# Packing the 257-column spectral units of a fused FFT-filter and GEGLU kernel into 256 columns, with bursts of four and new hooks

## The chip, the cores and the metric

One NeuronCore of one Trainium2 chip. The metric is device microseconds of one execution, median of several. All comparisons are of runs in the fast state, except where said (granted clock 0.997 to 1.0 in the runs recorded as fast, 0.756 to 0.991 in those recorded as slow). In the profiles PE is TensorE (PEld its weight loads), DVE is VectorE, ACT ScalarE, POOL GpSimd and SP SyncE; L612 is line 612 of the kernel.

## The reference

```python
x  = A_x                                   # (1, 2048, 512) bf16
xn = layernorm(x)                          # over the last axis
X  = rfft2(xn, axes=(-2, -1))              # 2048 x 257 complex
y  = irfft2(X * (w_r + 1j * w_i), s=(2048, 512))
g, u = xn @ w_gate, xn @ w_up              # 512 -> 1792
return x + y + (gelu(g) * u) @ w_down      # 1792 -> 512
```

## The kernel before

It is written engine by engine. A helper `op` appends an instruction to an engine's queue and works out the semaphore waits from named reads and writes. TensorE's program is the GEGLU (gate, up and down projections, in four blocks of 512 tokens). At fixed places between its matmul groups stand *hooks*, numbered 0 to 159, and a plan says which other work is issued at which hook. A hook is half a gate/up pair (0.86 us of PE) or a third of a down projection (1.0 us).

The filter is done by matmuls against DFT matrices, in 16 units at each of six stages. D transforms the feature axis. A does 64 points of the token axis, on two halves of 64 rows. A goes to a scratch array in DRAM and comes back as `tv`, transposed. B does 32 points, with two halves of 64 columns. VectorE multiplies by the filter. C transforms back, on 64-row halves, and goes through DRAM again to `vv`. E and F finish. A unit of A, B or C has 257 complex columns, so it takes two PSUM banks (the program's banks are 512 fp32 columns wide) and the units go in bursts of two.

```python
def load_tv(j):                                    # scratch -> tv, waits for scr1[j] to land
    dma("sp", tv[j::16], scr1[8*j:8*j+8, :].rearrange("p (x c) -> p x c", c=KD), r=[("scr1", j)], w=[("tv", j)])

def unit_C(h):                                     # unit_A and unit_B are alike
    bk = take(2, 0.3)                              # two neighbouring PSUM banks
    y = yy[h % 4]
    def fn(e):
        for ri in range(2):
            for hh in range(2):                    # two 64-row halves of the array, side by side
                ins = e.matmul(bank(bk + hh)[:, 0:257], cm[64*hh:64*hh+64, h, ri, :], y[64*hh:64*hh+64, ri, 0:KD],
                               start=(ri == 0), stop=(ri == 1), skip_group_check=True)
        return ins
    op("pe", fn, r=[("cm", h), ("yy", h % 4, 0), ("yy", h % 4, 1)], w=[("ps", bk), ("ps", bk + 1)])
    op("act", lambda e: e.activation(v4[:], pair(bk), ACT.Copy), r=[("ps", bk), ("ps", bk + 1)], w=[("vp", h % 4)])
    dma("sp", scr2...[h], v4[:], ...)              # and load_vv(h - 2) right behind it
    ...                                            # cut
# ... cut: column 256 of vv by a matmul of its own (unit_row), 32 x 64, a small DMA and 16 POOL copies

for m in range(1, 4):                              # layernorm, transposes, folds of block m
    a = (2, 14, 23)[m - 1]
    t = (13, 23, 33)[m - 1]
    for i in range(4):
        at(a + i, (ln_stat, 4*m + i))              # VectorE, needs x of the block
    at(a + 3, (ln_aggr, 4*m, 4))
    for i in range(4):
        at(a + 5 + i // 2, (ln_norm, 4*m + i))     # VectorE -> xn
    at(t, (trans, m, (0, 1), ...)); at(t + 1, (trans, m, (2, 3), ...))   # PE, needs xn
    at(t + 2, (butter, m, 0)); at(t + 3, (butter, m, 1))                 # the folds, VectorE, for D
for j in range(NJ):
    h = (9, 11, 13, 15, 19, 21, 23, 25, 28, 30, 31, 33, 38, 39, 40, 41)[j]
    at(h, (unit_D, j))
    if j % 2:
        at(h + 2, (unit_A, j - 1), (unit_A, j))
for i in range(0, 16, 2):
    at(57.5 + 2.6*i, (unit_B, i), (unit_B, i + 1))
    at(65.3 + 2.6*i, (unit_C, i), (unit_C, i + 1))
at(117, (unit_row,))
for j in range(NJ):
    at(117 + 2.25*j, (unit_E, j)); at(121 + 2.25*j, (unit_F, j))
```

## Time and profile before

| | before |
|---|---|
| time, median (lowest to highest) of three runs | 192.27 us (191.92 to 192.29) |
| span of the profile | 190.6 us |
| PE busy / DVE / ACT | 96% / 63% / 47% |

The page of the kernel before: the busy time of each engine with its share of the span and its instructions, and the shares of the chain of work that ended last.

```profile
PE 182.7 (96%) x1170; PEld 93.0 (49%) x1184; DVE 120.3 (63%) x316; ACT 88.6 (47%) x162; POOL 27.2 (14%) x54
...
PE 87%; DVE 5%; DMA 3%; issue 1%; SPq 1%; POOL 1%; ACT 0%; DVEq 0%
```

TensorE bounds the kernel (busy 96% of the span, 87% of the chain that ended last): only what takes a slot on PE or makes PE wait counts. The list of PE's waits (microseconds in total, times, longest):

```profile
PE ps L347 <- DVE gl L316: 1.2, 1, 1.2
PE ps L375 <- DVE xn L365: 1.1, 2, 0.6
PE ps L612 <- DMA wu<-in_B_w_up_dram: 0.9, 1, 0.9
PE ps L415 <- DVE arena L401: 0.6, 1, 0.6
PE ps L654 <- DVE m_1 L476: 0.2, 1, 0.2
PE ps L654 <- DVE hT L618: 0.2, 1, 0.2
```

The first and third lines, and half of the second, are the start. Waits come later: a D unit (L415) at 30.95 us for the fold, and the transposes of the third block (L375) at 35.83 us for `xn`. In the timeline of PE (columns are explained below; in brackets the idle time before, and what ended it):

```profile
30.95 0.23 PE L415 MATMUL ps<-fd,arena 128*128 128x128 f16 x1 [0.63 <-DVE arena L401]
35.83 0.56 PE L375 MATMUL ps<-ident,xn 128*128 128x128 f16 x7 [0.59 <-DVE xn L365]
```

The timeline of PE around a C burst. Columns: start in us, length in us, line, operation, result and inputs, stationary tile, shape, count.

```profile
119.52 1.03 PE L612 MATMUL ps<-xnT,wu 128*128 128x512 f16 x4
120.48 0.62 PE L490 MATMUL ps<-yy,cm 64*128 64x257 bf16 x8
121.03 1.04 PE L597 MATMUL ps<-xnT,wg 128*128 128x512 f16 x4
```

Read the starts here, not the lengths. A 512-column matmul follows another after 216 ns, so four take 0.86 us; from the first to the second line are 0.96 us. The eight matmuls of the burst are four side-by-side pairs of 257 columns, about 0.44 us at the 110 ns from one pair to the next; they take 0.55 us. Entering and leaving the 64-row mode costs about 0.1 us each time. In the trace's own nanoseconds it is 93 to 100 in all 24 bursts: an entry makes the slot of a 512-column matmul 309 to 312 instead of 216, an exit that of a burst's last matmul 201 to 206 instead of 106 (two exits read longer). The list of waits shows none of it.

### The profile page before, as it was taken

The numbers are of one execution on the slowest core, as the hardware profiler recorded it, in microseconds if no ns is written. First come the engines' busy times: TensorE is split into PE (matmuls) and PEld (weight loads), VectorE is DVE, ScalarE is ACT, GpSimd is POOL, SyncE is SP. The second block draws the span as 40 slices with busy tenths as digits, with TensorE's granted clock in tenths as the row PEclk, the third lists the DMA queues.
The fourth block names the chain that finished last, engine by engine and source line by source line (L and its number), as shares of the span: only waits on it lengthen the run. The fifth ranks groups of instructions, "written<-read, shape, count | busy, mean of one in ns | idle before, by whom it ended". The sixth has DMA issues, their size and how long they took to land.

```text
span 190.6 us, 3253 instructions
## 1 busy us (share of the span) xinstructions
PE 182.7 (96%) x1170; PEld 93.0 (49%) x1184; DVE 120.3 (63%) x316; ACT 88.6 (47%) x162; POOL 27.2 (14%) x54
## 2 busy tenths in 40 slices
PE   7699998899999999999999999999999999999993
PEld 2376554455555444444444444444445555555562
DVE  3679849888562142777557646723424969697781
ACT  1344555556447322355636364433225665646410
POOL 2300210417331000222230000000001110111100
PEclk9999999999999999999999999999999999999999
DMA  4999998366998850126765242235000222212112
GB/s 124 280 270 378 214 239 226 128 162 159 232 173 179 186 153 7 39 65 114 161 151 141 79 113 79 73 99 138 3 1 0 57 59 53 59 41 63 37 28 55
DMA packets 20239, 22.96 MB, mean 120 GB/s; under 512 B 2176, under 2 KB 18048, under 8 KB 19840
## 3 DMA queue, kind: packets, MB, share of 16 engines
q1 hardware_dynamic: 17056, 16.69, 33.2%
q0 software_dynamic: 1712, 5.22, 12.8%
q10 hardware_dynamic: 1456, 0.85, 1.6%
q8 instruction: 9, 0.15, 0.3%
q14 instruction: 6, 0.05, 0.1%
HBM read 16.44 MB, written 6.31 MB: 119 GB/s over the span
## 4 chain that ended last, share of the span: by engine, by line
PE 87%; DVE 5%; DMA 3%; issue 1%; SPq 1%; POOL 1%; ACT 0%; DVEq 0%
PE ps L597 24%; PE ps L654 24%; PE ps L612 24%; DMA wu<-in_B_w_up_dram 3%; PE ps L464 2%; PE ps L490 2%; PE ps L524 2%; PE ps L553 2%; PE ps L375 2%; PE ps L634 2%; PE ps L439 1%; SPq L304 1%; DVE hT L618 1%; DVE st L353 1%; PE ps L443 1%
## 5 line engine op out<-in xcount | busy, mean ns | idle before, releaser
L618 DVE TENSOR_TENSOR hT<-ps,gl 128x512 bf16<-128x512 f32 (+1 forms) x60 | 38.8, 651 | 34.1 <-PE ps L612 32.9
L612 PE MATMUL ps<-xnT,wu 128*128 128x512 f16 (+1 forms) x240 | 58.2, 365 | 0.9 <-DMA wu<-in_B_w_up_dram 0.9
L597 PE MATMUL ps<-xnT,wg 128*128 128x512 f16 (+1 forms) x240 | 58.4, 365 | 0.1
L600 ACT ACTIVATE gl<-ps 128x512 bf16<-128x512 f32 (+1 forms) x60 | 34.1, 569 | 47.1 <-PE ps L597 46.2
L654 PE MATMUL ps<-wd,hT 128*128 128x512 bf16 x196 | 47.4, 379 | 1.0 <-DVE m_1 L476 0.2
L612 PEld LDWEIGHTS ps<-xnT,wu 128*128 128x128 bf16 x240 | 22.3, 98 | 22.1 <-DMA wu<-in_B_w_up_dram 1.2
L597 PEld LDWEIGHTS ps<-xnT,wg 128*128 128x128 bf16 x240 | 22.4, 98 | 21.5 <-issue 1.9
L654 PEld LDWEIGHTS ps<-wd,hT 128*128 128x128 bf16 x210 | 19.5, 98 | 22.4 <-issue 1.7
L669 DVE TENSOR_TENSOR x_sb<-ps,x_sb 128x512 bf16<-128x512 f32 x12 | 8.2, 687 | 12.1 <-PE ps L654 12.1
L559 ACT ACTIVATE eo<-ps 128x512 bf16<-128x512 f32 x16 | 9.5, 596 | 13.4 <-PE ps L553 13.4
L532 POOL COPY zt<-xn 1x128 bf16<-1x128 bf16 x16 | 4.8, 298 | 75.9 <-DMA xn<-row 44.8
L353 DVE BATCH_NORM_STATS2 st<-x_sb 128x6 f32<-128x512 bf16 x16 | 10.8, 685 | 3.6 <-DMA x_sb<-in_A_x_dram 3.6
L422 ACT ACTIVATE xs<-ps 128x512 f16<-128x512 f32 x16 | 9.6, 598 | 7.5 <-PE ps L418 7.5
L470 ACT ACTIVATE xc<-ps 128x514 f16<-128x514 f32 x16 | 8.7, 600 | 8.0 <-PE ps L464 8.0
L449 ACT ACTIVATE tt<-ps 128x514 f16<-128x514 f32 x16 | 8.7, 598 | 7.6 <-PE ps L443 7.6
L496 ACT ACTIVATE vp<-ps 128x514 bf16<-128x514 f32 x16 | 8.7, 598 | 5.8 <-PE ps L490 5.8
L531 ACT ACTIVATE zt<-ps 128x512 bf16<-128x512 f32 x16 | 9.5, 592 | 0.0
L361 POOL TENSOR_TENSOR rstd<-vpe,mhalf 128x4 f32<-128x4 f32 (+2 forms) x6 | 5.0, 835 | 25.2 <-DVE vpe L360 25.2
L308 POOL DMA_DIRECT2D Wr<-in_A_w_r_dram x8 | 5.0, 629 | 21.7 <-PE ps L612 16.5
L365 DVE TENSOR_SCALAR xn<-x_sb,ag,rstd 128x512 f16<-128x512 bf16 x16 | 6.0, 420 | 2.3 <-POOL rstd L361 2.3
L385 DVE COPY xnT<-ps 128x1024 f16<-128x1024 f16 (+2 forms) x8 | 4.8, 604 | 3.4 <-PE ps L375 3.4
L553 PEld LDWEIGHTS ps<-gm,zt 128*128 128x128 bf16 x64 | 4.9, 98 | 3.8
(65 smaller groups left out, 168.4 us busy)
## 6 DMA issues: line engine op xcount, KB each, us to landing
scr<-tt SPq DMA_DIRECT2D x16, 128.5 KB
tv<-scr SPq DMA_DIRECT2D x16, 128.5 KB
scr<-vp SPq DMA_DIRECT2D x16, 128.5 KB
arena<-scr SPq DMA_DIRECT2D x16, 128.5 KB
out_dram<-osb SPq DMA_DIRECT2D x30, 64.0 KB
x_sb<-in_A_x_dram SPq DMA_DIRECT2D x6, 256.0 KB, 12.6
Wr<-in_A_w_r_dram POOLq DMA_DIRECT2D x8, 128.5 KB, 3.9
Wi<-in_A_w_i_dram POOLq DMA_DIRECT2D x8, 128.5 KB, 4.6
```

Of the source, the lines that this page charges most:

```text
L353: op("dve", lambda e: e.bn_stats(st[:, j, :], x_sb[:, j, :]), r=[("x", j, 0), ("x", j, 1)], w=[("st", j)])
L422: op("act", lambda e: e.activation(x4[:].rearrange("p (a c r) -> p a c r", a=2, r=4), bank(bk).rearrange("p (a r c) -> p a c r", a=2, r=4) ...
L449: op("act", lambda e: e.activation(t4[:], pair(bk), ACT.Copy, scale=SC_A), r=[("ps", bk), ("ps", bk + 1)], w=[("tt", j % 4)])
L470: op("act", lambda e: e.activation(xc[s2][:, :, 0:KD], pair(bk), ACT.Copy, scale=SC_B), r=[("ps", bk), ("ps", bk + 1)], w=[("xc", s2)])
L531: op("act", lambda e: e.activation(z[:], bank(bk).rearrange("p (a c) -> p a c", a=4), ACT.Copy, scale=SC_E), r=[("ps", bk)], w=[zk])
L553: ins = e.matmul(o[:, i // 2, i % 2, :], z[:, i, :], gm[:, i, :], start=(i == 0), stop=(i == 3), skip_group_check=True)
L559: op("act", lambda e: e.activation(o2[:], bank(bk), ACT.Copy), r=[("ps", bk)], w=[ok])
L597: ins = e.matmul(bank(bg)[:, 0:n], wg_sb[:, dc, fc * P:(fc + 1) * P], xnT[:, dc, c0:c0 + n], start=(dc == 0), stop=(dc == 3))
L600: op("act", lambda e: e.activation(gl[k % 3][:, 0:n], bank(bg)[:, 0:n], ACT.Gelu_apprx_tanh), r=[("ps", bg)], w=[("gl", k % 3)])
L612: ins = e.matmul(bank(bu)[:, 0:n], wu_sb[:, dc, fc * P:(fc + 1) * P], xnT[:, dc, c0:c0 + n], start=(dc == 0), stop=(dc == 3))
L618: op("dve", lambda e: e.tensor_tensor(hT[b % 2][:, fc, h0:h0 + n], bank(bu)[:, 0:n], gl[k % 3][:, 0:n], ALU.mult), r=[("ps", bu), ("gl", k ...
L654: ins = e.matmul(bank(bk), hT[b % 2][:, fc, jj * P:(jj + 1) * P], wd_sb[:, fc, :], start=(fc == 0), stop=(fc == NFC - 1))
```

## The change

After the transform of the feature axis, columns 0 and 256 are purely real, so one complex column can carry both, one as its real and one as its imaginary part. The change packs them into one ("kd 0 and 256 as one"): a unit then has 256 columns and fits one PSUM bank, so that A, B and C can go in bursts of four. To multiply the packed column by two different filter values it needs the column at negated frequency: tiny matmuls with a permutation matrix (15 of 2 to 8 columns) and 44 tiny VectorE operations. The row unit goes. Scratch reads get hooks of their own, and the hooks of layernorm, transposes and D move. The change also regroups the loads of the filter and of C's matrices into fewer ones and moves E and F to other hooks. The core of the diff, with cuts:

```diff
-        vp = [sb("vp%d" % i, [P, 2, KD], BF16) for i in range(4)]
+        tp = [sb("tp%d" % i, [P, 2, 2, KW], F16) for i in range(NTP)]      # KW = 256, NTP = 3
...
+        def quad_C(q):
+            bks = [take(1, 0.22) for _ in range(4)]
+            for i in range(0, 4, 2):
+                def fn(e, i=i):
+                    for u in range(2):
+                        for ri in range(2):
+                            for hh in range(2):
+                                ins = e.matmul(bank2(bks[i + hh])[:, u, :], cm[64 * hh:64 * hh + 64, hs[i + u], ri, :],
+                                               y[64 * hh:64 * hh + 64, i + u, ri, :], start=(ri == 0 and u == 0), ...)
+                    return ins
+                op("pe", fn, ..., w=[("ps", bks[i]), ("ps", bks[i + 1])])    # ScalarE is released pair by pair
...
-            a = (2, 14, 23)[m - 1]
-            t = (13, 23, 33)[m - 1]
+            a = (2, 15, 26)[m - 1]
+            t = (13, 25, 34)[m - 1]
...
-            h = (9, 11, 13, 15, 19, 21, 23, 25, 28, 30, 31, 33, 38, 39, 40, 41)[j]
+            h = (9, 11, 13, 15, 20, 22, 24, 26, 30, 32, 33, 34, 40, 41, 42, 43)[j]
             at(h, (unit_D, j))
-            if j % 2:
-                at(h + 2, (unit_A, j - 1), (unit_A, j))
+            if j % 4 == 3:
+                at(h + 2, (units_A, j - 3, 4) if j < 12 else (units_A, 14, 2))
+                for i in range(j - 3, j + 1):
+                    at(h + (7 if j < 12 else 2), (load_tv, i))
+            elif j == 13:
+                at(h + 2, (units_A, 12, 2))
+        for q in range(4):
+            b = CB + BS * q                                  # 59 + 9 q
+            at(b, (quad_B, q))
+            for s in range(4):
+                at(b + 1 + 2 * s, (quad_mul, q, s))
+            at(b + 2, (filter_cols, q))
+            at(b + 6, (quad_neg, q))
+            at(b + 8, (quad_col, q))
+            at(b + CD, (quad_C, q))                          # CD = 12
+            for h in QUADS[q]:
+                at(b + CD + (5 if q < 3 else 0), (load_vv, h))
-        at(117, (unit_row,))
+            at(CE + EF * j, (unit_E, j))                     # 112 + 2.45 j, F four hooks later
```

## The prediction

> **What bounds it now.** TensorE. The first part of the page gives PE 182.7 us busy of a 190.6 us span (96%), DVE 63%, ACT 47%, and the chain that ended last is 87% PE. The clock is full. From the starts in the timeline, back-to-back matmuls follow each other in columns/2.4 GHz plus about 3 ns (216 ns for 512 columns, 56 ns for 128). The view of waits has only 4.2 us for PE in all: 2.9 us in the warm-up and first loads, 0.6 us for the folds (a D unit, 30.95 us), 0.6 us of 1.1 for the layernorm of the third block (transposes at 35.83 us), 0.2 us twice for DVE.
>
> **The hidden cost.** The 64-row (A, C) and 64-column (B) units run as 24 bursts of two units. Each entry (512-column matmul to the next start: 309-312 ns instead of 216) and each exit (203-206 ns instead of about 110) loses 96-99 ns, so about 0.193 us a burst, 4.6 us in all. No wait shows it. [...]
>
> **The change, costed.**
> - 24 bursts become 13 (A: three of four units, two of two; B and C: four each): 11 x 0.193 = -2.1 us on PE.
> - The row unit for column 256 goes: 0.18 us slot plus 0.10 us entry, -0.27 us. Its 16 POOL copies were off the path.
> - 257 -> 256 columns: about -0.03 us.
> - Added: 15 matmuls of 2 to 8 columns, full-array mode. An estimate from the 56 ns slot of a 128-column matmul with its own weights: +0.9 us.
> - Added: 44 tiny DVE ops. At the 150-170 ns of tiny ones here, +7 us of DVE in the B/C stretch, where 9 hooks replace 10.4 per four units: about 9.3 us of DVE work in a 10.4 us period. Off the path, barely.
> - D of the second block one hook later (20 for 19), the third block's transposes two later with its statistics one later: a hook is 0.86 us of PE, so both 0.6 us waits should go: -1.2 us.
> - A 4-unit burst puts 2.2 us of evictions before the next gelu; PE should not notice. A(14,15) sits about one ACT eviction behind D(15): +0.1-0.3 us. Other new bank or DVE waits: allow +0.4 us.
> - tv: last A and first B both move two hooks, keeping the present slack (landed 73.1, used 75.8 us). vv: 14 hooks (about 12.5 us) between last C and first E instead of 16; landing took 8.7 us and I expect about 10. No wait.
>
> Sum: -2.1 -0.3 -1.2 -0.2 (the two DVE waits, partly) +0.9 +0.6 = about -2.3 to -2.5 us.
>
> **Prediction: 189.8 us (range 188.7 to 191.3).** Faster by over 2%: 0.07; within 2%: 0.90; slower: 0.03.
>
> **What would show it.** 13 entries and exits at about 97 ns each and no row unit; PE busy about 180-181 us; the waits on L401's fold and the third block's xn gone from PE's view; tiny matmuls with slots near 56 ns; DVE near 67% with 85-95% in the B/C windows; no DMA among PE's releasers after the start-up; the tail after the last matmul still about 3 us.
>
> **What would make it wrong.** DVE falling behind in B/C so that up-projection banks come late (several PE waits on hT multiplies); bursts of four holding PSUM so that gates wait for ACT; B or E waiting for scratch reads now issued in fours; [...] the layernorm waits merely moving to the fourth block.

Two passages that no trace of this case shows are cut, where marked. "The clock is full" is a granted clock of 1.000 in the profile of before, and the 2.4 GHz is the slope between the two slots named there (160 ns more for 384 more columns). The two allowances for new waits (+0.1-0.3 and +0.4 us) were estimates of mine that no trace or run had shown.

## More of the kernel before

The timeline of VectorE before the first late wait:

```profile
25.06 0.69 DVE L385 COPY xnT<-ps 128x1024 f16<-128x1024 f16 x1 [1.20 <-PE ps L375]
27.15 0.69 DVE L353 BATCH_NORM_STATS2 st<-x_sb 128x6 f32<-128x512 bf16 x1 [1.40 <-DMA x_sb<-in_A_x_dram]
27.76 0.67 DVE L618 TENSOR_TENSOR hT<-ps,gl 128x512 bf16<-128x512 f32 x1
28.35 0.68 DVE L397 TENSOR_TENSOR arena<-xnT 128x1024 f16<-128x1024 f16 x1
28.95 0.68 DVE L398 TENSOR_TENSOR arena<-xnT 128x1024 f16<-128x1024 f16 x1
...
30.48 0.42 DVE L401 TENSOR_TENSOR arena<-arena 128x512 f16<-128x512 f16 x1
```

The first statistic of the third block (L353) stands at hook 14 and waits 1.40 us for its x to land. The fold of the second block (L397 to L401, hooks 15 and 16) stands behind it in the queue though its own data is there.

## The result, and the profile after

| | before | after |
|---|---|---|
| time, median (lowest to highest) of four runs | 192.09 us (191.91 to 192.29) | 187.74 us (187.51 to 188.17) |
| ratio, 95% interval | | 0.9776 (0.9751 to 0.9800) |
| span of the profile | 190.6 us | 185.7 us |

A ratio is the mean time of one kernel's fast runs over that of the other's of the same rounds, so it is not quite the ratio of the medians. The change won 4.35 us; 2.4 us were predicted, and 187.74 lies below the range. It is faster by over 2%, to which the prediction gave 0.07.

The page of the kernel after, the same lines:

```profile
PE 181.3 (98%) x1198; PEld 95.4 (51%) x1198; DVE 124.5 (67%) x360; ACT 87.7 (47%) x161; POOL 16.4 (9%) x29
...
PE 93%; DMA 3%; SPq 1%; DVE 0%; issue 0%
```

The list of PE's waits is down to one line, the wait for the first memset (a write of zeros by VectorE):

```profile
PE ps L364 <- DVE gl L331: 1.2, 1, 1.2
```

The timeline of PE around a C burst, as above. L527 are two of the tiny matmuls.

```profile
107.50 0.18 PE L527 MATMUL ps<-Wr,be 128*128 128x8 bf16 x1
107.53 0.17 PE L527 MATMUL ps<-Wi,be 128*128 128x8 bf16 x1
107.55 1.02 PE L694 MATMUL ps<-xnT,wu 128*128 128x512 f16 x4
108.51 1.05 PE L583 MATMUL ps<-yq,cm 64*128 64x256 bf16 x16
109.49 1.04 PE L679 MATMUL ps<-xnT,wg 128*128 128x512 f16 x4
```

Four units take 0.98 us from entry to exit, plus 0.1 us of the entry: 1.08 us. Twice the burst of two above is 2 x (0.55 + 0.10) = 1.30 us. And a tiny matmul, though recorded with 0.17 us, holds PE for 0.03 us.

The timeline of VectorE in the early stretch:

```profile
25.15 0.68 DVE L414 TENSOR_TENSOR arena<-xnT 128x1024 f16<-128x1024 f16 x1
25.75 0.69 DVE L415 TENSOR_TENSOR arena<-xnT 128x1024 f16<-128x1024 f16 x1
26.99 0.69 DVE L370 BATCH_NORM_STATS2 st<-x_sb 128x6 f32<-128x512 bf16 x1 [0.55 <-DMA x_sb<-in_A_x_dram]
27.60 0.41 DVE L417 TENSOR_TENSOR arena<-arena 128x512 f16<-128x512 f16 x1
27.92 0.42 DVE L418 TENSOR_TENSOR arena<-arena 128x512 f16<-128x512 f16 x1
```

The x of the third block lands as late as before (27 us), but the first half of the fold now stands ahead of the statistic that waits for it, and D and the transposes come later in PE's program.

The load of VectorE in a whole period of B and C, by the view of windows (microseconds, then busy time and instructions of each engine, the granted clock, DMA share and GB/s):

```profile
94.00:105.00 11.00, 11.00 (x79) 5.36 (x79) 8.92 (x33) 5.83 (x12) 0.00 (x0) 1.00 0.39 110
```

VectorE is busy 81% (8.92 of 11.00 us; 85 to 95% were predicted), and PE 100%.

**A ledger of PE.** PE is full, so the time from its first to its last start can be split without a rest, start to start: what a matmul needs when nothing holds it up (0.4167 ns a column + 2.7 ns, the line through the 216 ns of 512 columns and the 56 ns of 128 in these traces, where 256 columns take 109; the tiny matmuls are not on it and are counted by their slots) and what is lost beyond. From the two traces:

| PE, us | before | after | difference |
|---|---|---|---|
| A, B, C units with all entries and exits | 15.60 | 13.17 | -2.43 |
| row unit with its entry | 0.27 | 0 | -0.27 |
| tiny matmuls (15 slots of 26 to 29 ns) | 0 | 0.41 | +0.41 |
| losses of the start, to 13.5 us | 3.64 | 2.96 | -0.68 |
| late waits (795 + 751 + 168 ns) | 1.71 | 0 | -1.71 |
| from the last matmul's start to the end | 3.27 | 3.29 | +0.02 |

The third late wait, 168 ns, stands before a D unit at 43.2 us; the list of waits doesn't show it. The sum is -4.66 us of the 4.88 between the spans. About 0.1 us of the rest is the first matmul after each exit: of 512 columns it holds PE for 225 to 227 ns instead of 216 (19 times before, 12 after), of 128 columns for 66 or 67 instead of 56 (4 and 1); what is left is scattered in small excesses. The medians are only 4.35 us apart: the profiled run of before took 192.7 us, more than any of the four timed ones, and single profiles contain a start that differs by run, which the experiments take up.

### The profile page after: what moved, and what is told of

Read it like the earlier page. It is cut to its first block, busy times and chain, and to the rows that moved or that the text cites. A ratio compares the mean times of both kernels' runs of the same rounds, so it can differ in the third digit from the quotient of the medians.

```text
span 185.7 us, 3290 instructions
## 1 busy us (share of the span) xinstructions
PE 181.3 (98%) x1198; PEld 95.4 (51%) x1198; DVE 124.5 (67%) x360; ACT 87.7 (47%) x161; POOL 16.4 (9%) x29
## 4 chain that ended last, share of the span: by engine, by line
PE 93%; DMA 3%; SPq 1%; DVE 0%; issue 0%
PE ps L694 26%; PE ps L679 26%; PE ps L736 24%; DMA wu<-in_B_w_up_dram 3%; PE ps L461 2%; PE ps L495 2%; PE ps L583 2%; PE ps L608 2%; PE ps L635 2%; PE ps L392 2%; PE ps L716 2%; SPq L319 1%; PE ps L435 1%; PE ps L434 1%; PE ps L432 1%; PE ps L433 0%
## 5 line engine op out<-in xcount | busy, mean ns | idle before, releaser
L736 PE MATMUL ps<-wd,hT 128*128 128x512 bf16 x210 | 49.6, 379 | 0.0
L751 DVE TENSOR_TENSOR x_sb<-ps,x_sb 128x512 bf16<-128x512 f32 x11 | 7.6, 688 | 10.6 <-PE ps L736 10.6
L439 ACT ACTIVATE ring<-ps 128x512 f16<-128x512 f32 x16 | 9.5, 596 | 6.2 <-PE ps L435 6.2
L470 ACT ACTIVATE tp<-ps 128x512 f16<-128x512 f32 x16 | 8.4, 600 | 5.5 <-PE ps L461 5.5
L591 ACT ACTIVATE tp<-ps 128x512 bf16<-128x512 f32 x16 | 8.3, 602 | 3.4 <-PE ps L583 3.4
L501 ACT ACTIVATE ring<-ps 128x512 f16<-128x512 f32 x16 | 8.2, 610 | 0.0
L649 DVE TENSOR_TENSOR eh<-eo 128x256 bf16<-128x256 bf16 x16 | 4.6, 290 | 4.6 <-ACT eo L641 4.4
L364 PE MATMUL ps<-gl 128*128 128x512 bf16 (+1 forms) x17 | 6.1, 516 | 1.2 <-DVE gl L331 1.2
```

The lines of the kernel that those rows point to most:

```text
L439: op("act", lambda e: e.activation(x4.rearrange("p (a c r) -> p a c r", a=2, r=4), bank(bk).rearrange("p (a r c) -> p a c r", a=2, r=4), A ...
L470: op("act", lambda e, i=i, b=b, k=k: e.activation(tp[k][:, b], bank2(bks[i + b]), ACT.Copy, scale=SC_A), r=[("ps", bks[i + b])], w=[("tp", ...
L591: op("act", lambda e, i=i, hh=hh, k=k: e.activation(vp[k][:, hh], bank2(bks[i + hh]), ACT.Copy), r=[("ps", bks[i + hh])], w=[("tp", k, hh)])
L736: ins = e.matmul(bank(bk), hT[b % 2][:, fc, jj * P:(jj + 1) * P], wd_sb[:, fc, :], start=(fc == 0), stop=(fc == NFC - 1))
```

## The experiments

The theory after the result: the gain is on PE alone, namely fewer changes of tiling mode (2.3 us), the hooks (1.7 us or more), and nothing is given back, because tiny matmuls are cheap and nobody waits. The main rival: bursts of four and fewer operations shorten waits of the other engines, and the modes are a side show. Fourteen runs were made (two of them of the unedited kernels), all with the right result.

### The new hooks alone, on the kernel before

```diff
-            a = (2, 14, 23)[m - 1]
-            t = (13, 23, 33)[m - 1]
+            a = (2, 15, 26)[m - 1]
+            t = (13, 25, 34)[m - 1]
-            h = (9, 11, 13, 15, 19, ...)[j]
+            h = (9, 11, 13, 15, 20, ...)[j]          # the list of after
-            at(57.5 + 2.6 * i, ...B...); at(65.3 + 2.6 * i, ...C...)
+            at(59 + 2.6 * i, ...B...);   at(66.8 + 2.6 * i, ...C...)
```

> The kernel before, with only the new hooks for layernorm, transposes and D units (A follows D; B and C one and a half hooks later so that tv keeps its slack). Ledger theory: the three late waits (795, 751 and 168 ns, counted start to start) go, so -1.7 us, about 190.4 us, and no late PE wait is left. The prediction's sizing from the idle column: -1.2 us, about 190.9 us. Rival, that the bursts of four are what removed those waits: no gain, about 192.

Measured: 190.75 us, ratio 0.9914 (0.9843 to 0.9985), so -1.65 us by the ratio and -1.3 us by the medians, on a chip whose runs scattered more. The interval (-3.0 to -0.3 us) holds both sizings, -1.7 and -1.2, so the times don't tell them apart; that there is no gain, as the rival had it, lies outside. In the trace the late losses fall by 1.40 us: 0.31 us are left (169 ns at a D, 143 ns at the fourth block's transposes). The expectation that no late wait is left was a little too good.

This trace also settles the two "waits on DVE" of 0.2 us. In the kernel before, the down projection after a B burst shows nine matmuls where the program has ten there:

```profile
93.34 0.64 PE L464 MATMUL ps<-tv,be 128*64 128x257 f16 x8
94.14 2.11 PE L654 MATMUL ps<-wd,hT 128*128 128x512 bf16 x9 [0.16 <-DVE hT L618]
96.18 0.62 PE L490 MATMUL ps<-yy,cm 64*128 64x257 bf16 x8
96.73 1.04 PE L654 MATMUL ps<-wd,hT 128*128 128x512 bf16 x4
```

9 + 4 = 13 of the 14 matmuls of a down projection. In the trace of this experiment all 14 are recorded (5 + 9), and the burst is left at the usual cost, with no wait:

```profile
91.08 1.24 PE L654 MATMUL ps<-wd,hT 128*128 128x512 bf16 x5
92.25 0.63 PE L464 MATMUL ps<-tv,be 128*64 128x257 f16 x8
92.82 2.12 PE L654 MATMUL ps<-wd,hT 128*128 128x512 bf16 x9
```

The "wait" was one lost record: its excess over the usual exit, 223 ns (220 ns at the other "wait"), is about a 512-column slot (216 ns). In all, the first trace of before shows 196 of the 210 512-column down-projection matmuls.

### The old hooks on the kernel after

The same edit the other way round (B and C keep their hooks).

> The kernel after, with the old hooks for layernorm, transposes and D units. Ledger theory: the late waits return, +1.5 to +1.7 us, about 189.3 us. Rival, that bursts of four removed them: about 187.8 us and no late wait.

Measured: 189.66 us, ratio 0.9860 (0.9786 to 0.9934), near the +1.5 to +1.7 expected (0.9860 against 0.9776 for after, which ran on another chip, is 1.6 us). But only one late loss is back, 757 ns at the third block's transposes; the D unit did not wait, and the start lost 4.08 us where the trace of after had 2.96. That did not fit the picture of fixed losses and led to the pin tested below.

### Tiny matmuls after the bursts, and inside them

```diff
+        def tiny():                                  # four full-array matmuls of 8 columns, result unused
+            bt = take(1, 0.12, 0.1)
+            ... e.matmul(bank(bt)[:, 0:8], ident[:], fd[:, 0:8], start=True, stop=True, ...) x 4
 # first kernel: tiny() right after each of the 11 bursts of four; second: after the burst's first two units
```

> The kernel after, with four full-array matmuls of 8 columns put right after each of the 11 bursts of four: 44 more tiny matmuls, no more mode changes. At the 26-29 ns slots that the trace of after shows: +1.2 us, about 188.9 us. At the 56 ns that the prediction used: +2.5 us, about 190.2 us. Rival, that such work hides off the path: under +0.3 us.

> The same 44 tiny matmuls, but in the middle of each of the 11 bursts, so that each burst is left and entered once more. Mode-change theory: 11 x (2 x 97 + 11 to 24 ns) = +2.3 us over the run with the tinies after the bursts, about 191.2 us. Rival, that long bursts gain by what they do to the other engines' waits and not by mode changes: within 0.4 us of the run with the tinies after.

Measured, on one chip: 188.84 us after the bursts (ratio 0.9812, 0.9742 to 0.9881) and 191.21 us inside (0.9951, 0.9864 to 1.0038). The timelines of PE around the same C burst, first after, then inside:

```profile
109.27 1.05 PE L598 MATMUL ps<-yq,cm 64*128 64x256 bf16 x16
110.25 0.26 PE L456 MATMUL ps<-fd,ident 128*128 128x8 f16 x4
110.36 1.02 PE L696 MATMUL ps<-xnT,wg 128*128 128x512 f16 x4
```

```profile
111.54 0.61 PE L598 MATMUL ps<-yq,cm 64*128 64x256 bf16 x8
112.08 0.26 PE L456 MATMUL ps<-fd,ident 128*128 128x8 f16 x4
112.27 0.61 PE L598 MATMUL ps<-yq,cm 64*128 64x256 bf16 x8
112.81 0.39 PE L696 MATMUL ps<-xnT,wg 128*128 128x512 f16 x1
```

The same 20 matmuls take 1.09 us from entry to exit in the first (110.36 - 109.27) and 1.27 us in the second. Eleven extra exits and entries cost 2.4 us of the time, as the mode theory had it, and the rival, which allowed 0.4 us, fell. And 44 tiny matmuls cost 1.1 us over after's 187.74 (on another chip; 0.7 us by the two ratios): 59 of them take 1.67 us of slots in the trace, 28 ns each, half of the 56 ns predicted.

### Packed columns with bursts of two

```diff
-            at(b, (quad_B, q))
+            at(b, (quad_B, q, 0)); at(b + 2, (quad_B, q, 1))        # two units each
-            at(b + CD, (quad_C, q))
+            at(b + CD - 2, (quad_C, q, 0)); at(b + CD, (quad_C, q, 1))
-            # A: bursts of 4, 4, 4, 2, 2
+            # A: eight bursts of 2, after every second D
```

> The kernel after, packed into 256 columns with its new hooks, but with bursts of two units: A after every second D, B and C in two halves two hooks apart; 24 bursts again. Mode-change theory: 11 more bursts at 0.193 us plus 11 to 24 ns for the first pair of each: +2.2 to +2.3 us over after, about 190.0 us, no late PE wait. Rival, that packing the columns is itself worth most of the gain: under 188.5 us.

Measured: 191.24 us, ratio 0.9961 (0.9938 to 0.9983). That is 3.5 us over two other variants of after on the same chip (187.7 us), where 2.3 were expected. A, B and C with entries and exits take 15.45 us in its trace: packing alone is worth 0.15 us (15.60 before), the long bursts 2.28 us (13.17 after). So packing pays only by what it allows. The expectation was wrong by 1.2 us: 0.44 us are new late waits (a D unit and the fourth block's transposes), and the start lost 3.92 us in this trace against 2.7 to 3.7 in the traces of after and of its variants with the new hooks. The list of PE's waits puts 1.1 us of that to one load, the gate weights:

```profile
PE ps L679 <- DMA wg<-in_B_w_gate_dram: 1.1, 1, 1.1
```

All four of its runs took long (190.8 to 191.4), so chance alone is a poor account; but only one was traced, and why its start should differ is open.

### Scratch reads with their bursts, and one release for a burst

```diff
 # first kernel
-                    at(h + (7 if j < 12 else 2), (load_tv, i))
+                    at(h + 2, (load_tv, i))
-                at(b + CD + (5 if q < 3 else 0), (load_vv, h))
+                at(b + CD, (load_vv, h))
 # second kernel: the matmuls of a burst of A, B or C as one op, so one release of ScalarE for all four units
```

> The kernel after, with the scratch reads issued at the hook of their burst and not five hooks later. Ledger theory: the reads are off PE's path, within 0.3 us of after, about 187.8 us. Rival, that reads waiting for the landing of the writes block the queue for the next writes, so that ScalarE and then PE wait: over +1 us and late PE waits on ScalarE.

> The kernel after, with one release of ScalarE at the end of each burst of four instead of one for each pair (B: for each unit). The first eviction starts about 0.5 us later. Ledger theory: banks have the slack, +0 to +0.3 us, at most 188.0 us. Rival, that the early release is what keeps gates and the next burst from waiting: over +1 us with PE waits on ScalarE.

Measured, on one chip: 188.11 us (ratio 0.9805, 0.9762 to 0.9848) and 187.73 us (0.9782, 0.9750 to 0.9813). Neither trace has a late loss on PE of over 25 ns. These two parts of the change gain nothing that these runs resolve; the reads' own hooks may be worth up to 0.4 us, within the scatter.

### The last four A units as one burst

```diff
-                at(h + 2, (units_A, j - 3, 4) if j < 12 else (units_A, 14, 2))
+                at(h + 2, (units_A, j - 3, 4))
-            elif j == 13:
-                at(h + 2, (units_A, 12, 2))
```

> The kernel after, with the last four A units in one burst at the hook of the second pair: 12 bursts for 13. Mode-change theory: -0.2 us if nothing waits, about 187.5 us. The change's own choice of two pairs says that something would wait: the burst behind the eviction of D(15), or B behind tv landing later: +0.2 us or more over that.

> The last four A units as one burst once more, beside the kernel after on the same chip: 0.2 us under it if mode changes are all there is (ratio about 0.999 of after), which five rounds may not resolve; no late PE wait in the trace.

Measured: 187.70 us at first (ratio 0.9780), then, beside after, 188.05 us in its five fast runs (0.9788, 0.9747 to 0.9828) against 187.78 us. A, B and C take 12.96 us in the trace, 0.2 us less as expected, and nothing waits, but the times don't show it. This is no better version by the clock; the change's "two pairs" was not needed either.

### After and before once more

Both kernels unedited.

> The kernel after once more, only to see how far its start-up wait for the first weights moves from run to run: time 187.4 to 188.2 us; PE's excess in the first 13.5 us, 2.96 us in the first trace, anywhere from 2.7 to 4.1 us; no late wait; 26 mode changes of 94-99 ns.

> The kernel before once more, for a second trace. Missing-record theory: the two 0.2 us waits on DVE at 94.1 and 115.2 us are lost matmul records and are not at the same place in a trace that has all 210 of the 512-column down-projection matmuls; the waits at the second block's fold and the third block's transposes are there again, together 1.2 to 1.8 us.

Measured: after 187.78 us, ratio 0.9779 (0.9747 to 0.9811), the result again; its start lost 3.37 us, it has no late wait and 26 mode changes. The single run of before (its state is unknown) took 192.21 us. Its trace lost the same 14 down-projection records, so the two 0.2 us "waits" are there again, at the same places; it can't test the theory of lost records, the trace of the new hooks did. (The other twelve lost records leave gaps of 215 or 216 ns too, at other places of the first trace.) Its two late losses were 244 and 755 ns, 1.0 us together, less than the 1.2 I expected at least.

### One statistic one hook later

```diff
-            a = (2, 14, 23)[m - 1]
+            a = (2, 15, 23)[m - 1]                   # on the kernel before, nothing else
```

> The kernel before with one number changed: the statistics and normalisation of the third block one hook later, so that the first statistic, which waits for that block's x to land at about 27 us, stands behind the first fold of the second block in VectorE's queue and not ahead of it. Queue theory: the 795 ns before the D unit goes; the transposes then come earlier and wait 0.2 to 0.8 us for xn; together -0.8 to -1.3 us, about 191.0 us. Rival, that later statistics only make xn later: the wait of the transposes grows by as much, about 192.0 us.

Measured: 192.10 us, ratio 1.0001 (0.9963 to 1.0039). My theory fell. The D unit's wait is gone, as the order of the queue says, but nothing is won. Two lines from the list of PE's waits in this trace (the others are the first memset and the two lost records):

```profile
PE ps L375 <- DVE xn L365: 0.8, 1, 0.8
PE ps L612 <- DMA wu<-in_B_w_up_dram: 0.6, 1, 0.6
```

The transposes took the wait over (927 ns start to start). Across the four traces then at hand with the old hook of these transposes, their first one starts at 35.83, 35.36, 35.56 and 35.21 us, whatever PE lost earlier. That suggests a pin: x lands at about 27 us, statistics, `rstd` and normalisation follow, and PE meets `xn` at about 35.5 us.

For three of the four the traces show the pin. The first statistic of the third block, which waits for x, starts at 27.15 and 26.67 us in the two traces of before and at 26.52 us in after with the old hooks; the first transpose follows 8.68, 8.68 and 8.69 us later. In the trace of this experiment that statistic stands behind the fold, starts at 28.09 us with no wait for x, and the first transpose follows 7.47 us later: here VectorE's order sets the time, not the landing. The statistic in after with the old hooks, and here:

```profile
26.52 0.69 DVE L370 BATCH_NORM_STATS2 st<-x_sb 128x6 f32<-128x512 bf16 x1 [1.02 <-DMA x_sb<-in_A_x_dram]
28.09 0.69 DVE L353 BATCH_NORM_STATS2 st<-x_sb 128x6 f32<-128x512 bf16 x1
```

### Useless work early, on both kernels

```diff
+        at(6, (extra,))            # three 512-column matmuls into a spare bank, 0.65 us of PE, at about 18 us
```

> The kernel before with three useless 512-column matmuls (0.65 us of PE) at hook 6, about 18 us. Pin theory: the waits at the second block's fold and the third block's transposes shrink by as much; the third block's first transpose starts at 35.2 to 35.9 us as before; time within 0.2 us of before, about 192.2 us. Rival, that the waits are just two fixed losses: +0.65 us, about 192.8 us.

> The kernel after with the same three matmuls at hook 6. Both theories: no slack on PE, +0.65 us over after, about 188.4 us; only if the pin is still there, within 0.2 us of after.

Measured: before with the extra work 192.04 us over its six fast runs, ratio 1.0001 (0.9967 to 1.0035): 0.65 us of PE work for nothing, though the interval reaches +0.67 us. After with the same work 188.52 us over its four fast runs, ratio 0.9829 (0.9781 to 0.9876) where after on this chip had 0.9779: +0.7 us by the medians, with intervals that overlap. Its trace shows the work in full: the span is 0.57 us longer than in the second trace of after, where the start lost 0.07 us more, and neither has a late wait. So the times fit the pin, which the 8.7 us above show: before the change, PE had slack in front of the third block's transposes; after it, none.

With this the start and the late waits before 60 us belong together. Their losses, start to start:

| kernel, hooks of the transposes | start | late | sum, us |
|---|---|---|---|
| before, twice; one statistic later; after with old hooks | 3.64, 3.76; 4.03; 4.08 | 1.71, 1.16; 1.09; 0.76 | 5.36, 4.92; 5.12; 4.84 |
| after, twice; before with new hooks | 2.96, 3.37; 2.92 | 0, 0; 0.31 | 2.96, 3.37; 3.23 |

With the old hooks the sum is 5.06 us on average, with the new 3.19: the hooks are worth about 1.9 us. (The other traces with the new hooks lost 2.7 to 3.7 us in all, except that of bursts of two, 3.92 + 0.44.) The start varies by run, in good part with a wait for the first weights: the lists of PE's waits give it 0.9 us in the first trace of before, none in that of after and 0.2 us in the second of after. Under the old hooks a lucky start was lost again at the pin.

## Why the prediction was wrong, point by point

The direction and the mechanism were right: PE bounds, modes cost what no list of waits shows, the early waits go, and nothing else was on the path. The steps that failed are terms of the sum, and nearly all in the same direction.

| term | predicted, us | measured, us |
|---|---|---|
| mode changes, 11 bursts fewer, and 257 to 256 columns | -2.1 | -2.43 |
| row unit | -0.3 | -0.27 |
| early waits at the fold and the third block's transposes | -1.2 | -1.65 (hooks alone, -3.0 to -0.3) to -1.9 (ledger) |
| the two DVE waits | -0.2 | 0, lost records |
| tiny matmuls | +0.9 | +0.41 |
| new waits: A(14,15) behind D(15), banks, DVE | +0.6 | 0 |
| sum | about -2.4 | -3.9 to -4.2; times: -4.35 |

- **"Other new bank or DVE waits: allow +0.4 us", and "+0.1-0.3 us" for A(14,15)**: one of the two largest misses (0.6 us; the early waits are the other). Not one late wait is in the trace of after. VectorE had the load that was counted (67% of the span as predicted, 81% in B and C) and still met every bank in time. An allowance for the unknown was booked as if it were a cost.
- **"An estimate from the 56 ns slot of a 128-column matmul"**: the slots are 26 to 29 ns. The trace of before has no matmul of fewer than 64 columns, so the estimate carried the 56 ns over to 2 to 8 columns unmeasured.
- **"both 0.6 us waits should go: -1.2 us"**: mis-sized twice. The idle column counts from the recorded end of a matmul: a 512-column one is recorded with 379 ns while the next starts after 216, so each wait reads 163 ns too short (0.63 for 795 ns, 0.59 for 751). And the waits were the visible part of a pin that also ate good starts.
- **"11 x 0.193 = -2.1 us"**: right for what it counts (2.29 us of entries and exits went, with the row unit's two). Each burst also has a longer first pair (117 ns in A and C, 130 ns in B, against 106), and units of 257 columns a longer pair (110 to 111 ns against 105 to 106).
- **Right**: 13 entries and exits at 93 to 99 ns, the row unit, no DMA among the late releasers, the tail of 3.3 us, DVE at 67%. PE busy came out at 181.3 us (180 to 181 predicted), but that number is a poor witness, since it counts what records are there.

What stays open: the start of the bursts-of-two kernel, and 0.05 to 0.3 us of the 4.35 that neither the terms above nor the 0.1 us of first matmuls after an exit hold.

## What to carry to other kernels

When PE is full, make a ledger of its starts, not of its waits: here changes of tiling mode cost 93 to 100 ns each without a name, a wait read 163 ns too short after a 512-column matmul, and a lost record read as a wait (0.2 us, twice). Before pricing an early wait, ask what absolute time pins it: here 0.65 us more work before a wait whose end was set by a load left the time as it was (ratio 1.0001, 0.9967 to 1.0035), and moving its consumer behind it was worth 1.9 us by the ledger where the list of waits showed 1.2. Book unknown new waits as a wider range, not as a cost in the middle of the sum.
